# A first quarter of x loaded a second time for its statistics, GpSimd's shuffles with the lower half first, and a new order of the work on every engine

## The chip, the cores and the metric

The kernel runs on one core of one Trainium2 chip. The metric is device time in microseconds (us) of one execution, inputs and output in HBM. Lower is better.

## The reference

One block of a sequence model, with S = 2048 positions and D = 448 channels, all inputs bf16. A long convolution over the sequence is done by FFT, its result gates the normalized input, and an MLP that mixes positions follows.

```python
def _A_ref(q, k, v, shift_k, ssm_k, ssm_D):          # q = layernorm(x)
    k_shift = sum(k_pad[:, t:t+S, :] * shift_k[:, 3-t] for t in range(4))
    kv  = k_shift * v
    y   = irfft(rfft(pad(kv)) * rfft(pad(ssm_k)))[:S]   # length 2S, along the sequence
    return q * (y + kv * ssm_D)

def _B_ref(x, w1, b1, w2, b2):                        # F = 1792, positions are mixed
    u = gelu(einsum("bsd,sf->bdf", layernorm(x), w1) + b1)
    return (einsum("bdf,fs->bds", u, w2) + b2).transpose(0, 2, 1)

x  = A_q
h  = x + _A_ref(layernorm(x), A_k, A_v, A_shift_k, A_ssm_k, A_ssm_D)
h2 = h + _B_ref(layernorm(h), B_w1, B_b1, B_w2, B_b2)
```

## The kernel before

**Layout.** A position s is 16*q + r: q is the partition (128 of them), r the row (16). x, k, v and the output lie in one arena of SBUF as 16 rows of 448 channels per partition. PSUM has 8 banks, and the FFT stages take them in pairs.

**Stages,** by the names that the kernel gives them (its `PLAN`):

- `tables` computes the sine tables; `loads` brings ssm_k, k, v and small vectors; `kT` and `kv.0` to `kv.8` transpose ssm_k and k on TensorE; `kv.9` to `kv.16` do the four-tap shift with diagonal matrices and multiply by v on VectorE (L983).
- `k1` (ssm_k) and `u1` (kv) are the first FFT stage: 16 steps each of 8 small matmuls (L1035), each evacuated from two PSUM banks to SBUF in one instruction (L1045, or L1043 for the first four of k1). Every second step sends three DMAs that move the data across partitions, here called shuffles: two from GpSimd's queue (8 partitions each) and one from SP's (16 partitions), L1051.
- `k2` and `u2` are the second FFT stage (L1070, evacuated at L714 to L718).
- `i1` multiplies the two spectra: 16 products on VectorE, 128x1792 each (L1136), and does the first inverse stage on TensorE (L1153); its results are evacuated (L714) and shuffled once more: two DMAs from GpSimd (lower and upper half of the partitions, L1176) and two from SP (two further rows) for each of seven pairs. The last pair, `i1.16`, goes out by four DMAs of its own: three on SP's queue and one on ScalarE's (L1165).
- `i2` is the second inverse stage, one pair of matmuls for each row r (L1275; rows 0 and 1 have four more, L1283). On its result the gate, both normalizations and the result Q of a row are worked out by VectorE, ScalarE and GpSimd.
- `mlp.0` to `mlp.15` multiply the first half of w1 by Q row by row (L1408, 7 matmuls a row, between the i2 matmuls); `mlp.17` to `mlp.23` the second half (L1418); `mlp.24` to `mlp.39` are w2 and the output (L1430).

Beside these run `xload` (x in four quarters, L891), `q` (mean and variance of each row of x, `bn_stats` at L1212, then `bn_aggr` at L1214, and two small GpSimd instructions for 1/sqrt), `xn` (rows 0 to 3 normalized by ScalarE, L1245), `ct` (transposes of the tables for i2), and `w1a`, `w1b`, `w2` (the weights, by SP). The four quarters of x land in the place of the shuffles' ring buffers, so they can't start before the last u1 shuffle has landed: that is `after=shuf["u"]` in `emit_xload`. `w1a.0` has that condition too; `w1a.1` to `w1a.3` wait for the four DMAs of `i1.16`.

**Order.** Each engine runs one list, written out in `ORDER`. A token such as `u2.11:4-5` means the operations 4 and 5 of step 11 of stage u2. `_Sched.schedule` replays the lists with a model of durations, which decides the interleaving in which waits are placed and which PSUM bank each step takes; the order on an engine is the list's. An engine never runs ahead of an instruction that waits.

**Names used below.** `i1.16:9` and `i1.16:18` evacuate the last inverse pair (both on ScalarE); `i1.16:19`, `:20`, `:22` are its DMAs on SP, `i1.16:21` the one on ScalarE. `i1.4:17` is the evacuation ahead of the last two GpSimd shuffles, `i1.4:18` and `i1.4:20`. `i2.1`, `i2.2`, `i2.9`, `i2.10` are rows 0 and 1 of the second inverse stage, `i2.17` row 2, the first whose data come from `i1.16`'s DMAs; `i2.3` to `i2.8` turn row 0 into Q, for which `mlp.0` waits.

The pieces of code that matter most:

```python
def emit_xload():
    for c in range(4):
        op("sp", lambda e, W, c=c: e.dma_start(X[:, 4*c:4*c+4, :], x2d[:, 4*c:4*c+4, :]),
           w=[(o_X + 4*c*DB, 4*DB)], dmab=128*4*DB, after=shuf["u"])
# emit_q, for each row r
op("dve", lambda e, W, bs=bs, r=r: e.bn_stats(out=bs, in_=X[:, r, :]), r=[(o_X + r*DB, DB)], w=[(ob, 24)], n=D, kind="1x")
```

Of the kernel before, what the change touches and what calls it, by code (L numbers as in the profile page):

```python
# [10 lines left out]
ENGS = ("pe", "act", "dve", "pool", "sp")  # L11
# [3 lines left out]
        "kT.3:9-11 kT.5:0-7 kT.2:4-7 kT.5:9-10 kT.6:0-7 kT.7:0-7 bias.0:0 kT.5:11 kv.7:0-7 k1.8:0-7 k1.9:0-7 "  # L15
        "k1.12:0-7 k1.10:0-7 kv.1:0-7 kv.2:0-11 k1.11:0-7 k1.15:0-7 k1.14:0-7 k1.13:0-7 kT.4:0-7 kv.8:0-11 "
        "kv.12:0-23 kv.9:0-27 kv.10:0-23 kv.11:0-27 k1.4:0-7 k1.0:0-1 u1.0:0-7 k1.0:2-7 u1.1:0-7 u1.2:0-7 k1.1:0-7 "
        "u1.3:0-7 kv.13:0-27 u1.4:0-7 k1.5:0-7 kv.14:0-23 k1.6:0-7 u1.6:0-7 k1.2:0-7 u1.5:0-7 kv.15:0-27 k1.7:0-7 "
        "u1.7:0-7 u1.8:0-7 u1.9:0-7 k1.3:0-7 k2.0:0-3 k2.1:0-3 k2.12:0-3 k2.13:0-3 k2.4:0-3 k2.5:0-3 kv.16:0-23 "
        "k2.9:0-3 k2.8:0-3 u1.10:0-7 u1.12:0-7 u1.13:0-7 u1.14:0-7 u1.15:0-7 u1.11:0-7 k2.2:0-3 k2.3:0-3 k2.6:0-3 "  # L20
        "k2.7:0-3 k2.10:0-3 k2.11:0-3 k2.15:0-3 k2.14:0-3 u2.0:0-3 u2.1:0-3 u2.13:0-3 u2.12:0-3 u2.8:0-2 u2.9:0-3 "
        "u2.8:3 u2.7:0-3 u2.6:0-3 i1.1:1-7 i1.1:10-16 i1.1:8 i1.1:17 i1.14:10-16 i1.14:1-7 i1.14:17 i1.14:8 "
        "i1.8:1-7 i1.8:10-17 i1.8:8 ct0.0:0-7 u2.10:0-3 u2.11:0-3 i1.10:1 i1.10:10-17 i1.10:2-8 u2.4:0-3 u2.5:0-3 "
        "i1.12:1-8 i1.12:10-17 u2.3:0-3 u2.2:0-3 i1.6:1-8 i1.6:10-17 u2.15:0-3 u2.14:0-3 i1.4:9-15 i1.4:0-7 i1.4:16 "
        "i1.16:1-7 i1.16:10-17 i1.16:8 ct.1:0-7 ct.0:0-7 ct.2:0-7 warm.0:0 i2.1:0-1 i2.2:0-3 i2.9:0-1 i2.10:0-3 "
        "i2.17:0-1 i2.45:0-1 i2.32:0-1 i2.20:0-1 i2.54:0-1 i2.28:0-1 warm.1:0 i2.41:0-1 mlp.0:1 mlp.0:4 mlp.0:2 "
        "mlp.0:0 mlp.0:6 mlp.0:3 i2.58:0-1 mlp.0:5 mlp.1:6 mlp.1:5 mlp.1:4 mlp.1:1 mlp.1:0 mlp.1:3 mlp.1:2 "
        "i2.67:0-1 mlp.2:3 mlp.2:2 mlp.2:1 mlp.2:5-6 mlp.2:4 mlp.2:0 mlp.3:4-5 mlp.3:2 mlp.3:1 mlp.3:3 mlp.3:0 "
        "mlp.3:6 i2.71:0-1 mlp.4:4 mlp.4:2 mlp.4:1 mlp.4:5 mlp.4:3 mlp.4:6 mlp.4:0 i2.80:0-1 mlp.5:1-2 mlp.5:4 "
        "mlp.5:6 mlp.5:5 mlp.5:0 mlp.5:3 i2.84:0-1 mlp.6:0 mlp.6:6 mlp.6:1 mlp.6:5 mlp.6:2 mlp.6:4 mlp.6:3 "  # L30
        "i2.93:0-1 mlp.7:6 mlp.7:0-1 mlp.7:5 mlp.7:3-4 mlp.7:2 mlp.8:2 mlp.8:6 mlp.8:5 mlp.8:3-4 mlp.8:0-1 mlp.9:3 "
        "mlp.9:1 mlp.9:6 mlp.9:0 mlp.9:5 mlp.9:4 mlp.9:2 i2.97:0-1 mlp.10:3 mlp.10:0 mlp.10:2 mlp.10:4-6 mlp.10:1 "
        "mlp.11:0 mlp.11:3 mlp.11:2 mlp.11:5 mlp.11:4 mlp.11:6 mlp.11:1 mlp.12:4 mlp.12:1 mlp.12:3 mlp.12:5 "
        "mlp.12:0 mlp.12:6 mlp.12:2 mlp.13:5 mlp.13:2 mlp.13:0 mlp.13:6 mlp.13:3 mlp.13:1 mlp.13:4 mlp.14:3 "
        "mlp.14:0 mlp.14:2 mlp.14:1 mlp.14:5 mlp.14:4 mlp.14:6 mlp.15:5 mlp.15:1 mlp.15:6 mlp.15:0 mlp.15:3 "
        "mlp.15:2 mlp.15:4 mlp.17:0-15 mlp.18:0-15 mlp.19:0-15 mlp.20:0-15 mlp.21:0-15 mlp.22:0-15 mlp.23:0-15 "
# [18 lines left out]
        "tables.7:7 kv.5:8 kT.5:8 kT.2:8 kT.7:8 kT.6:8 bias.1:0 kv.7:8 k1.12:8 kv.1:8 kv.2:12 kv.0:4 kT.4:8 kv.8:12 "  # L55
        "kv.12:24-25 kv.9:28-29 kv.10:24-25 kv.11:28-29 k1.0:8 k1.1:8 u1.3:8 kv.13:28-29 kv.14:24-25 k1.2:8 "
        "kv.15:28-29 u1.7:8 k1.3:8 k2.1:5 k2.5:4 kv.16:24-25 k2.9:5 u1.10:8 u1.11:8 k2.3:4 k2.7:4 k2.11:5 k2.15:5 "
        "u2.1:5 i1.0:0 i1.1:0 i1.14:0 i1.13:0 i1.7:0 i1.8:0 i1.9:0 i1.10:0 ct0.0:8 q.1:2 q.1:0 i1.11:0 i1.12:0 "
        "q.1:1 q.1:3 u2.5:5 i1.5:0 q.2:0 i1.6:0 i1.3:0 i1.2:0 q.2:1-2 q.3:0 i1.15:0 xn.0:1 q.2:3 i1.16:0 q.3:2 "
        "q.3:1 q.3:3 q.5:0 q.5:2 q.5:1 q.4:2 q.5:3 q.7:0 q.4:0 q.4:3 q.4:1 q.7:2 xn.3:1 q.6:0 q.6:2 q.6:1 q.6:3 "  # L60
        "i2.3:0 i2.4:0 i2.11:0 i2.5:0 i2.18:0 i2.6:0 i2.12:0 i2.21:0 i2.13:0 i2.8:0 i2.14:0 i2.55:0 i2.30:0 i2.16:0 "
        "i2.34:0 i2.43:0 i2.26:0 q.7:3 q.7:1 i2.47:0 i2.27:0 q.8:2 q.8:0 q.8:3 q.8:1 i2.39:0 i2.56:0 i2.40:0 "
        "i2.73:0 i2.60:0 i2.69:0 i2.52:0 i2.82:0 i2.85:0 i2.53:0 i2.86:0 i2.65:0 i2.66:0 i2.78:0 i2.79:0 i2.95:0 "
        "i2.98:0 i2.99:0 i2.92:0 i2.91:0 i2.105:0 i2.104:0 mlp.24:14 mlp.25:14 mlp.26:14 mlp.27:14 mlp.28:14 "
        "mlp.29:14 mlp.30:14 mlp.31:14 mlp.32:14 mlp.33:14 mlp.34:14 mlp.35:14 mlp.36:14 mlp.37:14 mlp.38:14 "
        "mlp.39:14 mlp.39:30 "
# [110 lines left out]
class _Sched:  # L177
# [50 lines left out]
    def op(self, W, fn, r=(), w=(), br=(), bw=(), n=0, kind=None, est=None, dmab=None, keng=16, rate=None, after=(), safter=(), mode=0):  # L228
# [3 lines left out]
        o = _Op()  # L232
# [90 lines left out]
    def schedule(self):  # L323
        ops = self.ops
        n = len(ops)
# [23 lines left out]
        free_at = {e: 0.0 for e in ENGS}  # L349
        fab = 0.0  # L350
        mode = 0
        events = []
        t = 0.0
        done = 0
        finish = [0.0] * n
        start = [0.0] * n
        INF = 1e18

        def can_acquire(o):
            need = {}  # L360
            for b in o.acq:
                need[b.pool] = need.get(b.pool, 0) + b.k
# [196 lines left out]
def _build(nc, A_q, A_k, A_v, A_shift_k, A_ssm_k, A_ssm_D, B_w1, B_b1, B_w2, B_b2, out):  # L559
# [11 lines left out]
    DB = 2 * D  # L571
# [921 lines left out]
```

## Time and profile before

| | us |
|---|---|
| median of the runs shown | 175.15 (174.36 to 175.57) |
| the profiled execution, its own time | 173.93 |
| its span | 172.1 |
| from the start to the first product of the spectra | 50.43 |
| from there to the landing of the last shuffle | 28.24 |
| from there to the end of the span | 93.4 |

| engine | busy us | share of the span | instructions |
|---|---|---|---|
| TensorE (PE) | 161.4 | 94% | 1419 |
| VectorE (DVE) | 102.7 | 60% | 190 |
| ScalarE (ACT) | 90.1 | 52% | 130 |
| GpSimd (POOL) | 59.0 | 34% | 152 |

Busy time is an average over stages with different limits; the stages are read one by one below. A matmul in the profile is counted busy from its issue to its modelled end, so that matmuls overlap: one of 448 columns is shown at about 0.35 us, and the next starts 0.19 us after it. Evacuations that follow each other overlap in the same way: one of 128x896 lasts 0.91 us on ScalarE and 1.08 on VectorE, and the next begins 0.80 and 1.00 us after it.

### The profile page before, as it was taken

The page shows a single profiled execution, that of the slowest core. Times are in us where ns is not written, and L with a number is a line of the kernel's source. Part 1 is how long each engine was busy: PE and PEld are TensorE (multiplying, and loading weights), DVE is VectorE, ACT ScalarE, POOL GpSimd, SP SyncE. Part 2 cuts the span into 40 slices and gives each one's busy share as a digit, 9 for nine tenths or more (in the row PEclk, how much of TensorE's full clock was granted, in tenths as well). Part 3 has the DMA queues.
Part 4 walks back from the last instruction along what each step waited for, and adds up shares of the span by engine and source line. Part 5 has one row for each costly group of instructions (what it writes and reads, how often), then busy time and mean ns, then how long its engine had stood idle before and what let it go on. Part 6 is the DMA issues. An engine that isn't in the chain of part 4 may idle for free.

```text
span 172.1 us, 3562 instructions
## 1 busy us (share of the span) xinstructions
PE 161.4 (94%) x1419; PEld 93.4 (54%) x1419; DVE 102.7 (60%) x190; ACT 90.1 (52%) x130; POOL 59.0 (34%) x152
## 2 busy tenths in 40 slices
PE   6999999979999998759999999999999999999994
PEld 2676745433333433333454555555567777777783
DVE  7998899868979999999999550000003132132231
ACT  3696757798999999989958345421210000000000
POOL 8344817690820546664898740000000000000000
PEclk9999999999999999999999999999999999999999
DMA  5999765783749677655599999993000111101111
GB/s 157 416 289 386 275 203 212 298 333 127 224 109 342 251 195 240 200 170 145 162 363 396 403 421 424 411 425 157 0 0 4 53 53 53 53 0 57 53 53 53
DMA packets 15628, 35.15 MB, mean 204 GB/s; under 512 B 3740, under 2 KB 9740, under 8 KB 15612
## 3 DMA queue, kind: packets, MB, share of 16 engines
q1 hardware_dynamic: 12468, 28.25, 45.1%
q0 software_dynamic: 2880, 6.49, 12.0%
q8 instruction: 11, 0.18, 0.4%
q10 hardware_dynamic: 264, 0.18, 0.3%
q14 instruction: 5, 0.04, 0.1%
HBM read 22.05 MB, written 1.84 MB: 139 GB/s over the span
## 4 chain that ended last, share of the span: by engine, by line
PE 63%; DMA 12%; ACT 9%; DVE 8%; issue 2%; POOL 2%; SPq 1%; DVEq 0%; POOLq 0%
PE ps L1430 24%; PE ps L1408 12%; PE ps L1418 12%; DMA arena<-arena 7%; ACT arena L714 6%; DVE arena L1136 6%; DMA arena<-in_A_ssm_k_dram 5%; PE ps L1035 4%; PE ps L1275 3%; ACT arena L1045 2%; POOL arena L1051 2%; PE ps L1070 2%; PE ps L968 2%; PE ps L1014 2%; DVE arena L983 2%
## 5 line engine op out<-in xcount | busy, mean ns | idle before, releaser
L1433 DVE SCALAR_TENSOR_TENSOR arena<-ps,arena 128x448 bf16<-128x448 f32 (+2 forms) x17 | 11.1, 656 | 56.2 <-PE ps L1430 56.2
L1430 PE MATMUL ps<-arena 128*128 128x448 bf16 (+2 forms) x238 | 42.7, 342 | 0.0
L1430 PEld LDWEIGHTS ps<-arena 128*128 128x128 bf16 x238 | 33.3, 145 | 9.5
L714 ACT CAST arena<-ps 128x896 bf16<-128x896 f32 (+1 forms) x31 | 25.0, 955 | 0.6 <-PE ps L911 0.3
L1045 ACT CAST arena<-ps 128x896 bf16<-128x896 f32 x23 | 19.5, 913 | 6.7 <-PE ps L1035 5.9
L1408 PE MATMUL ps<-arena 128*128 128x448 bf16 x112 | 22.5, 353 | 0.0
L1051 POOL DMA_DIRECT2D arena<-arena x32 | 17.5, 553 | 12.4 <-ACT arena L1045 11.8
L1418 PE MATMUL ps<-arena 128*128 128x448 bf16 x112 | 21.4, 352 | 0.0
L1398 ACT ACTIVATE arena<-ps,arena 128x448 bf16<-128x448 f32 x14 | 8.3, 637 | 18.1 <-PE ps L1418 14.4
L1136 DVE TENSOR_TENSOR arena<-arena 128x1792 bf16<-128x1792 bf16 x16 | 16.6, 1085 | 1.0 <-DMA arena<-arena 0.9
L1070 PE MATMUL ps<-arena 128*64 128x448 bf16 x128 | 15.5, 360 | 1.8 <-DMA arena<-arena 1.0
L1153 PE MATMUL ps<-arena 64*128 64x448 bf16 x128 | 14.9, 351 | 2.1 <-POOL arena L1232 0.9
L1418 PEld LDWEIGHTS ps<-arena 128*128 128x128 bf16 x112 | 11.0, 98 | 10.2
L1408 PEld LDWEIGHTS ps<-arena 128*128 128x128 bf16 x112 | 10.8, 98 | 10.6 <-DVE arena L1361 0.7
L1035 PE MATMUL ps<-arena 128*32 128x448 bf16 x256 | 15.1, 355 | 0.6 <-DVE arena L983 0.3
L1176 POOL DMA_DIRECT2D arena<-arena x14 | 8.3, 597 | 13.5 <-ACT arena L714 13.5
L1153 PEld LDWEIGHTS ps<-arena 64*128 64x128 f16 x128 | 5.9, 94 | 10.9 <-DVE arena L1136 3.7
L1070 PEld LDWEIGHTS ps<-arena 128*64 128x64 f16 x128 | 5.7, 108 | 10.7 <-ACT arena L715 2.6
L1275 PE MATMUL ps<-arena 128*128 128x448 bf16 x32 | 8.0, 353 | 2.1 <-DMA arena<-arena 1.9
L1330 ACT ACTIVATE arena<-arena 128x448 bf16<-128x448 f32 x14 | 8.0, 574 | 3.3 <-DVE arena L1302 3.1
L1035 PEld LDWEIGHTS ps<-arena 128*32 128x32 f16 x256 | 5.0, 95 | 8.4 <-DVE arena L983 2.6
L983 DVE TENSOR_TENSOR arena<-ps,arena 128x512 bf16<-128x512 f32 (+1 forms) x16 | 9.0, 617 | 0.8 <-PE ps L968 0.8
(96 smaller groups left out, 191.0 us busy)
## 6 DMA issues: line engine op xcount, KB each, us to landing
arena<-in_B_w_dram SPq DMA_DIRECT2D x8, 896.0 KB, 7.0
arena<-in_B_w_dram SPq DMA_DIRECT2D x2, 2048.0 KB, 17.0
arena<-arena SPq DMA_DIRECT2D x16, 224.0 KB, 3.4
arena<-arena POOLq DMA_DIRECT2D x32, 112.0 KB, 3.3
arena<-in_B_w_dram SPq DMA_DIRECT2D x2, 1536.0 KB, 19.1
arena<-arena POOLq DMA_DIRECT2D x14, 196.0 KB, 4.4
arena<-in_A_k_dram SPq DMA_DIRECT2D x4, 448.0 KB, 6.1
arena<-in_A_v_dram SPq DMA_DIRECT2D x4, 448.0 KB, 9.0
```

The source lines that it names most:

```text
L714: return e.copy(out=dst(), in_=src())
L983: return e.tensor_tensor(out=v, in0=u.rearrange("p t (r d) -> p t r d", d=64), in1=v, op=ALU.mult)
L1035: op("pe", lambda e, W, b=b, r=r, q=q, x=x, c0=c0: e.matmul(PS[32 * q:32 * q + 32, b.slots[x], 0:D], E[:, 2 * r + x, c0:c0 + 32], src[:, r ...
L1045: return e.copy(out=dst, in_=Ppair(b)) if W == "act" else e.tensor_copy(out=dst, in_=Ppair(b))
L1051: shuf[tag].append(op(q_, lambda e, W, g=g, i=i, a=a, nu=nu, jh=jh: e.dma_start(T[a + i:a + i + 4 * nu - 3:4].rearrange("p (j k) c d -> p ...
L1070: op("pe", lambda e, W, b=bs[h], h=h, j=j, c=c, par=par: e.matmul(PS[64 * par:64 * par + 64, b.slots[c], 0:D], FW[:, 64 * c:64 * c + 64], ...
L1136: op("dve", lambda e, W, m=m, i=i: e.tensor_tensor(out=MR(m.slots[0]).rearrange("p (x y) d -> p x y d", x=2), in0=TU[:, i].unsqueeze(2).br ...
L1153: k = op("pe", lambda e, W, b=bs[h], m=ms[h], par=par, t=t, tab=tab, xy=xy, P=P: e.matmul(Pb(b, par), tab[P, :], MR(m.slots[0])[P, xy, :], ...
L1275: k = op("pe", lambda e, W, b=b, r=r, h=h: e.matmul(Pb(b), ET[:, 2 * r + h, :], TZ[:, r, h, :], start=(h == 0), stop=(h == 1 and r >= NZ)) ...
L1408: op("pe", lambda e, W, r=r, fc=fc, b=bs[fc]: e.matmul(Pb(b), W1A[:, r, 128 * fc:128 * fc + 128], Q[:, r, :], start=(r == 0), stop=(r == R ...
L1418: op("pe", lambda e, W, r=r, fc=fc, b=b: e.matmul(Pb(b), W1B[:, r, 128 * (fc - n0):128 * (fc - n0) + 128], Q[:, r, :], start=(r == 0), sto ...
L1430: op("pe", lambda e, W, r=r, fc=fc, b=b, d0=d0, d1=d1: e.matmul(Pb(b)[:, d0:d1], W2[fc // 7][:, fc % 7, r:S:R], G[:, fc, d0:d1], start=(fc ...
```

## The change

1. A new stage `xe` loads the first quarter of x (rows 0 to 3, 448 KB) a second time, early, into rows 8 to 11 of the place of k, which are dead once k is transposed. The `bn_stats` of rows 0 to 3 read this copy; everything else still reads x where it was.
2. The lists of `ORDER` are new for all five engines, from about 12 us of the profile on. What moves:
   - from VectorE to ScalarE: the evacuations `kT.6:8`, `kv.8:12`, `u1.3:8`, `u1.7:8`, and the gates `i2.85:0`, `i2.98:0`; from ScalarE to VectorE: `k1.7:8`, `u2.11:5`, `i1.16:9`.
   - the `bn_stats` of rows 0 to 2 to between `k1.1:8` and `kv.13` (three in a row), that of row 3 to behind `u1.11:8`, with their `bn_aggr`.
   - GpSimd: `k1.11` ahead of `k1.9`, `k1.15` ahead of `k1.13`, `u1.3` ahead of `k1.5` and `k1.1`, `u1.15` ahead of `u1.11` (which was split around it); in i1 the lower half goes out first in every pair, `i1.1` leads, and the small instructions of rows 0 to 3 stand ahead of or among the first pairs.
   - SP: `xe.0` behind the first four shuffles; x's quarters in the order 2, 3, 1, 0; `i1.8` and `i1.10` early; `i1.16:20`, `:19`, `:22` in the place of `:22`, `:19`, `:20`; `w1a.0` behind `i1.16` and `i1.12:20` (it was behind the first two quarters of x); the left-over shuffles of i1 ahead of `w1a.1` to `w1a.3`, which follow each other.
   - TensorE: the order of a few steps in the first 16 us and in k2, u1, u2; `i2.41` ahead of `i2.54` and `i2.32`; the order of the seven matmuls in each row of the MLP.
3. The model in `schedule` has new constants for DMAs and latencies. It has no effect on the lists; it can change the bank that a step takes.

```diff
+        NE = 4
+        o_XE = o_KH + 8 * DB
+        XE = view(o_XE, [NE, D])
+        def emit_xearly():
+            for c in range(NE // 4):
+                sch.t0 = c
+                op("sp", lambda e, W, c=c: e.dma_start(XE[:, 4 * c:4 * c + 4, :], x2d[:, 4 * c:4 * c + 4, :]),
+                   w=[(o_XE + 4 * c * DB, 4 * DB)], dmab=128 * 4 * DB)
...
-                    op("dve", lambda e, W, bs=bs, r=r: e.bn_stats(out=bs, in_=X[:, r, :]), r=[(o_X + r * DB, DB)],
+                    op("dve", lambda e, W, bs=bs, r=r: e.bn_stats(out=bs, in_=XE[:, r, :] if r < NE else X[:, r, :]),
+                       r=[(o_XE + r * DB if r < NE else o_X + r * DB, DB)],
                        w=[(ob, 24)], n=D, kind="1x")
...
     "dve": (
-        ... k1.0:8 k1.1:8 u1.3:8 kv.13:28-29 kv.14:24-25 k1.2:8 kv.15:28-29 u1.7:8 k1.3:8 k2.1:5 k2.5:4 kv.16:24-25 k2.9:5 u1.10:8 u1.11:8 ...
-        ... i1.9:0 i1.10:0 ct0.0:8 q.1:2 q.1:0 i1.11:0 i1.12:0 q.1:1 q.1:3 u2.5:5 i1.5:0 q.2:0 i1.6:0 i1.3:0 i1.2:0 q.2:1-2 q.3:0 i1.15:0 xn.0:1 q.2:3 i1.16:0 q.3:2 ...
+        ... k1.0:8 k1.1:8 q.2:0 q.1:2 q.1:0 kv.13:29 kv.13:28 kv.14:25 kv.14:24 k1.2:8 k1.7:8 kv.15:29 kv.15:28 k1.3:8 k2.1:5 k2.5:4 kv.16:24-25 k2.9:5 u1.10:8 q.1:3 q.1:1 u1.11:8 q.2:2 q.2:1 ...
+        ... i1.10:0 i1.9:0 ct0.0:8 u2.11:5 i1.11:0 i1.12:0 u2.5:5 i1.5:0 i1.6:0 q.3:2 xn.0:1 i1.3:0 i1.2:0 xn.3:1 q.3:0 i1.15:0 i1.16:0 q.4:2 q.4:0 q.3:1 q.3:3 i1.16:9 ...
     "sp": (
-        ... k1.15:11 u1.1:11 ... xload.1:0 xload.0:0 w1a.0:0 xload.2:0 ct0.1:0-1 ... i1.16:22 i1.16:19-20 i1.12:22 i1.6:22 w1a.1:0 i1.4:21 ...
+        ... k1.15:11 xe.0:0 u1.1:11 ... xload.2:0 xload.3:0 ct0.1:1 ct0.1:0 xload.1:0 xload.0:0 ... i1.16:20 i1.16:19 i1.16:22 i1.12:20 w1a.0:0 i1.6:20 i1.6:22 i1.12:22 i1.14:22 i1.14:20 i1.1:20 i1.1:22 w1a.1:0 w1a.2:0 w1a.3:0 i1.4:21 ...
```

## The prediction

> **What bounds the kernel now.** I read the page first, then the chain of work that ended last, then busy time by stage. The chain shows who sets the end (start, length, engine, line; all in us).
>
> ```profile
> 46.25 4.15 DMA arena<-arena
> 50.41 0.02 issue
> 50.43 1.10 DVE arena L1136
> ...
> 59.26 1.06 DVE arena L1212 x2
> ...
> 62.50 3.17 ACT arena L714 x4
> 65.67 0.01 issue
> 65.69 4.87 ACT arena L714 x6
> ...
> 75.17 3.50 DMA arena<-arena
> 78.67 0.05 issue
> 78.72 0.94 PE ps L1275 x4
> ```
>
> Until 50.43 us the path runs through evacuations and shuffles and ends with the last u1 shuffle (4.15 us to land). Then VectorE (two of the moved `bn_stats` lie on the path), ScalarE's evacuations, the last shuffle of `i1.16` (landing at 78.67), and from there TensorE.
>
> ```profile
> 50.40:72.50 22.10, 19.81 (x176) 8.07 (x176) 22.02 (x32) 21.97 (x28) 9.39 (x18) 1.00 0.75 237
> 72.50:82.00 9.50, 7.43 (x54) 3.91 (x54) 8.99 (x29) 8.37 (x13) 5.40 (x11) 1.00 0.55 164
> 82.00:106.00 24.00, 24.00 (x128) 12.23 (x127) 17.23 (x48) 14.24 (x36) 15.96 (x38) 1.00 0.95 356
> ```
>
> The columns are length, then busy time of PE, PEld, DVE, ACT, POOL, the granted clock, the DMA share and GB/s. From 50.4 to 72.5 VectorE and ScalarE are both full, and TensorE nearly. From 82 to 106 TensorE alone is full: what comes after the first MLP matmul (81.86) is fixed. The time moves only by when `mlp.0` can start, and by stalls behind it.
>
> **Leg A, up to the first product (50.43).** The three `bn_stats` put behind `k1.1:8` take 3 x 0.53 us (the spacing of the pair at 59.18) of VectorE. Between 25.9 and 36.5 VectorE idles 1.8 us in all and loses `u1.3:8` and `u1.7:8` (1.00 each) for `k1.7:8` (1.00): room for 2.8, so they fit in total. But they stand ahead of `kv.13:29`. By my walk along the new lists with the durations of the old rows, `k1.1:8` ends at 26.99 (27.19 before), `kv.13:29` starts at 28.5 (28.11), `k1.2:8` ends at 31.7 (31.68), `k1.7:8` at 32.9 (33.71), `kv.15:28` at 34.5 (33.52), `k1.3:8` at 35.5 (35.73). `k2.0` waited for the landing of `k1.5:10` at 35.43; now it waits for `k1.1:10`, eighth in the same run of GpSimd's issues (issue about 31.0 against 30.67). So k2 starts 0 to 0.4 later by the issue, and up to 0.8 earlier if the landing takes nearer 4 than 4.76 us. From there both evacuating engines repeat the old lists. `u1.11:8` comes earlier (TensorE no longer waits for `u1.15`), and its `bn_aggr` and `bn_stats` (0.2 + 0.6) lie in the 0.8 us that VectorE idled before 43.21. The last GpSimd shuffle, `u1.11:10`, comes behind `u1.15`'s two, which wait for its evacuation at 44.51: 44.8 and three more issues of 0.54 is 46.4, against 46.25. Leg A: +0.1, bounds -0.8 (the last shuffle lands in 3.35 us like `u1.11:9`, not in 4.15) and +0.6.
>
> What the reordering must hide: GpSimd issues `k1.9` behind `k1.11` now, `k1.9:10` at about 21.2 instead of 18.00. `k1.0:8` (24.9) refills that buffer. Shuffles of that stretch land in 2.97 to 4.37 us, so at 24.2 to 25.6: a loss of 0 to 0.7 at VectorE, of which the 0.5 us before `k2.0` covers part (inside the +0.6).
>
> **The early load.** It is issued behind `k1.15:11`, at about 22.4 (`k1.15:8` now ends near 21.8, because ScalarE has `kv.8:12`, 0.90). VectorE asks for it at 26.9, so 4.5 us are free. The same 448 KB have a row:
>
> ```profile
> DMA to landing us min/median/max: 3.6/4.6/7.1
> ```
>
> Those are the four quarters of x. I take 4.3 (the second of them, issued beside another load): no stall. The bounds are 3.6 (nothing) and 7.1 (2.6 us of stall at the head of VectorE's queue, with `kv.13` and all of k1's and u1's evacuations behind it). [...]
>
> **Leg B, from the first product to the landing of `i1.16`.** Out of VectorE's list ahead of `i1.16:0` go five `bn_stats` (rows 0 to 3 and one of row 4), four `bn_aggr`: 1.09 + 0.16 + 0.54 + 0.60 + 0.53 + 0.09 = 3.0 us by the starts of what follows each. In come `u2.11:5` (1.07, as `u2.5:5`), two `bn_stats` of rows 4 and 5 (1.06) and a small one (0.1): 2.2. ScalarE loses `u2.11:5` (0.80). But TensorE hands out work no faster here: `i1.10:8` ends at 61.17 and `u2.5` at 62.05 in both. So ScalarE gains 0.4, not 0.8 (`u2.5:4` at 62.10, 62.50 before); from there its ten further evacuations run 0.80 apart, and `i1.4:17` starts at 70.17 (70.48). `i1.15:0` waits for `u2.15:4`, `i1.16:0` follows and ends at 70.95 (71.46): -0.5.
>
> Behind it, before: `i1.16:18` and `:9` in a row on ScalarE, the latter ending 2.97 us after `i1.16:0`; SP issues two more DMAs, and the last lands at 7.21. Now: `i1.16:9` on VectorE, behind two `bn_stats` and two `bn_aggr` (1.2), ends at 2.3. But SP's list has its two DMAs first and `:22` third: 2.33 + 2 x 0.71 + an issue to landing of 3.5 = 7.25. The parallel evacuation is eaten by the order of SP's queue. GpSimd's last pair follows `i1.4:17` (-0.3), lands at 75.8 (76.12), and TensorE's twelve matmuls of rows 0 and 1 then end just as `i1.16` lands. Leg B: -0.5, bounds -0.9 and 0.
>
> [...] GpSimd's issues in this stage last 587 to 666 ns beside two-input products, against 544 in the median in k1 and u1: 0.05 each, nothing on the path, and the last pair follows the last product. [...]
>
> **Leg C, up to `mlp.0`.** Row 0's Q is a chain: `i2.2` ends, three instructions on VectorE, one on GpSimd, then `i2.8`.
>
> ```profile
> 77.52 0.68 DVE L1312 SCALAR_TENSOR_TENSOR arena<-ps,arena 128x448 f32<-128x448 f32 x1 [0.47 <-PE ps L1283]
> ...
> 79.36 0.17 DVE L1321 BATCH_NORM_AGGREGATE arena<-arena 128x2 f32<-128x6 f32 x1
> ...
> 80.26 0.55 POOL L1354 TENSOR_TENSOR arena<-arena 128x1 f32<-128x1 f32 x1 [1.76 <-DVE arena L1350]
> ...
> 81.31 0.48 DVE L1361 TENSOR_SCALAR arena<-arena 128x448 bf16<-128x448 f32 x1
> ```
>
> It starts 0.3 earlier (77.2, after the pair's landing). The second `i2.11:0` now waits to 78.4 for row 1, and one `bn_aggr` more stands ahead of `i2.8`, which ends at 81.6 (81.80). TensorE, with the same 15 matmuls between `i2.17` and `mlp.0`, is ready at 81.4 and waits. So 0.3 of leg B's 0.5 is given back. And `w1a.0`, moved past 16 issues of SP (two quarters of x, six small ones of `ct0`, eight shuffles), is issued at about 76.1 instead of 51.28: 5.5 us before it is needed. Its kind lands in 4.8 to 6.35 us (`w1a.1` to `w1a.3`; it had a cover of 24 us before): from nothing to +0.85. I take 4.8, that of `w1a.1`, which was also issued behind small shuffles. `w1a.1` goes out at 81.5 (78.69) behind seven issues of 0.71, lands by 86.3 to 87.9, and `mlp.4` needs it at 88.0: just covered.
>
> **Sum.** A +0.1, B -0.5, C +0.3: -0.1; the MLP adds nothing. The profiled execution took 173.93 (span 172.1 and 1.8 around it), which becomes 173.8. The runs' median is 1.2 above that execution, so I forecast 175.0.
>
> **Rivals.**
> - *Landings and gaps fall well* (A -0.8, B -0.9, C half given back): -1.0 to -1.8, 173.2 to 174.1. For it: ScalarE and VectorE are full in B and lose 0.8 each. Against: the chain changes hands within 0.4.
> - *`w1a.0` comes late.* It decides when its landing exceeds 5.5 us; 6.2 is the median of its line. +0.5 to +0.9: 175.6 to 176.0.
> - *The early load stops VectorE* (slower). Place: `q.2:0` ahead of `kv.13`. It decides from a landing of 4.5 us. At the rows' 7.1 us, `kv.15:28` ends at 37.1, `k2.0` starts 1.7 later, and the whole path with it; with `k1.9:10` late as well 2.2: 176.7 to 177.3. Against: the DMA share is 0.76 there, not full.
> - *The change doesn't relieve the path at all*: B 0, C 0, because TensorE hands out the work at the old times; +0.1, 175.2.
>
> **How the numbers follow.** Forecast and the last rival together 0.58 (0.46 and 0.12), well-falling landings 0.16, `w1a.0` 0.13, the early load 0.13. About 1% (1.75 us) is what a measurement can tell from no change. Faster by more needs all of the first rival: 0.09. Slower by more is the early load and the tail of `w1a.0`: 0.15. The range takes in the first rival's middle and the foot of the third: 173.6 to 176.6.
>
> **What would show it.** The first product still near 50.5; `bn_stats` gone from 59 to 69 but two; `i1.16:0` ending at 71.0; the last landing at 78.2; TensorE idle 0.3 to 0.5 before `mlp.0` and nowhere behind it. Wrong if VectorE idles at 27 waiting for a DMA, if `mlp.0` or `mlp.4` waits for w1, or if the first product moves by over 0.8.

## The result, and the profile after

The changed kernel takes 176.01 us (median of 20 runs, 174.46 to 177.40) against 175.01 for the kernel before: a ratio of 1.0064, 95% interval 1.0039 to 1.0089. It is slower by 1.0 us, 0.6%, where no change was forecast (175.0); the time is inside the range of 173.6 to 176.6. The ratios here and below leave out runs more than 1.5% above the fastest of their kernel (one of these 20, and five of the twelve of after_w1a, a variant below). The profiled execution took 176.74 us (span 174.9), 2.8 more than that of the kernel before. So 1.8 of the 2.8 belongs to these two executions and not to the change; the first task is to tell the two apart.

Part of it is there from the start: `kv.12`, the first of TensorE's shift steps, begins at 19.92 us here and at 19.43 before, ahead of the early load's issue (22.55). In the 18 profiles of this document that start lies between 19.12 and 20.78, so two profiles can differ by half a us in absolute times without any effect of what comes later.

The chain of work that ended last, of the changed kernel (start, length, engine, line; us):

```profile
22.55 6.20 DMA arena<-in_A_q_dram
29.32 1.14 DVE arena L1248 x2
...
49.60 9.82 ACT arena L739 x12
...
70.20 1.79 ACT arena L739 x2
72.28 0.58 POOL arena L1212
72.86 3.95 DMA arena<-arena
...
78.85 1.49 PE ps L1320 x4
80.34 1.79 PE ps L1312 x6
...
84.08 0.92 PE ps L1445 x4
```

The early load stands on the path, which it was not to do. It lands 6.20 us after its issue. Then ScalarE's evacuations lead for 10 us without a break, and the last link before the second inverse stage is now a GpSimd shuffle (`i1.4:20`), not one of `i1.16`'s. The four matmuls of L1320 take 1.49 us at 78.85. The first MLP matmul comes at 84.06 (81.86 before).

VectorE around the load (start, length, operation, and the idle time ahead with what ended it):

```profile
26.89 1.08 DVE L1079 TENSOR_TENSOR arena<-ps,arena 128x896 bf16<-128x896 f32 x1
28.77 1.68 DVE L1248 BATCH_NORM_STATS2 arena<-arena 128x6 f32<-128x448 bf16 x3 [0.80 <-DMA arena<-in_A_q_dram]
30.37 0.67 DVE L1019 TENSOR_TENSOR arena<-ps,arena 128x512 bf16<-128x512 f32 x1
```

The kernel before at the same place:

```profile
27.11 1.08 DVE L1045 CAST arena<-ps 128x896 bf16<-128x896 f32 x1
28.11 2.00 DVE L983 TENSOR_TENSOR arena<-ps,arena 128x512 bf16<-128x512 f32 x3
```

VectorE waits 0.80 us for the load, works 1.6 us on statistics, and `kv.13`, whose matmuls end at 28.58, begins behind them at 30.37 (28.11 before). `k2.0` starts at 36.75 (35.47). The shuffles issued beside the load land late too: `k1.15:10` in 6.53 us (3.63 before).

The three stages of the prediction's second view (length, busy time of PE, PEld, DVE, ACT, POOL, granted clock, DMA share, GB/s), and then the same view second by second:

```profile
50.40:72.50 22.10, 20.44 (x183) 8.40 (x184) 21.32 (x26) 21.86 (x28) 10.43 (x18) 1.00 0.66 200
72.50:82.00 9.50, 7.14 (x47) 3.75 (x45) 8.04 (x23) 6.04 (x9) 3.54 (x7) 0.82 0.62 192
82.00:106.00 24.00, 23.77 (x123) 11.34 (x122) 18.09 (x52) 17.00 (x40) 17.07 (x40) 1.00 0.99 370
```

```profile
77.00:78.00 1.00, 1.00 (x7) 0.49 (x5) 0.77 (x3) 1.00 (x2) 0.14 (x1) 1.00 0.53 166
78.00:79.00 1.00, 1.00 (x4) 0.40 (x3) 0.76 (x2) 1.00 (x3) 0.92 (x2) 0.55 0.67 127
79.00:80.00 1.00, 1.00 (x4) 0.46 (x3) 0.55 (x1) 0.77 (x1) 0.22 (x1) 0.50 0.99 315
80.00:81.00 1.00, 1.00 (x4) 0.42 (x3) 0.62 (x2) 0.00 (x0) 0.00 (x0) 0.50 0.96 340
81.00:82.00 1.00, 1.00 (x6) 0.43 (x5) 0.88 (x5) 0.22 (x1) 0.04 (x1) 0.74 0.57 215
```

The granted clock reads 0.82 where it was 1.00. In fact it is 0.50 from 78.1 to 81.5, and the matmuls of rows 0 to 3 follow each other after 0.37 us instead of 0.19. Ahead of it TensorE idled for the last shuffle, here and, for less time, in the kernel before:

```profile
76.85 0.55 PE L1312 MATMUL ps<-arena 128*128 128x448 bf16 x2 [2.36 <-DMA arena<-arena]
```

```profile
76.17 0.55 PE L1275 MATMUL ps<-arena 128*128 128x448 bf16 x2 [1.90 <-DMA arena<-arena]
```

Row 0's chain is late by all of this; the lines that answer to those of before:

```profile
78.20 0.68 DVE L1349 SCALAR_TENSOR_TENSOR arena<-ps,arena 128x448 f32<-128x448 f32 x1 [0.43 <-PE ps L1320]
...
80.98 0.17 DVE L1358 BATCH_NORM_AGGREGATE arena<-arena 128x2 f32<-128x6 f32 x1
...
83.52 0.48 DVE L1398 TENSOR_SCALAR arena<-arena 128x448 bf16<-128x448 f32 x1
```

Q of row 0 is done at 84.00. `w1a.0` landed at 83.69, so in this execution its lateness is hidden behind the lower clock and nobody waits for it.

### The profile page after: what moved, and what is told of

Read it like the earlier page. It is cut to its first block, busy times and chain, and to the rows that moved or that the text cites. A ratio compares the mean times of both kernels' runs of the same rounds, so it can differ in the third digit from the quotient of the medians.

```text
span 174.9 us, 3563 instructions
## 1 busy us (share of the span) xinstructions
PE 163.5 (93%) x1419; PEld 94.1 (54%) x1419; DVE 102.0 (58%) x187; ACT 92.3 (53%) x133; POOL 59.9 (34%) x152
## 4 chain that ended last, share of the span: by engine, by line
PE 62%; ACT 13%; DMA 10%; DVE 9%; POOL 2%; issue 1%; SPq 1%; DVEq 0%; POOLq 0%
PE ps L1467 24%; PE ps L1445 12%; PE ps L1455 12%; ACT arena L739 9%; DMA arena<-in_A_k_dram 5%; PE ps L1106 4%; DMA arena<-in_A_q_dram 4%; PE ps L1312 3%; ACT arena L1081 3%; PE ps L1071 3%; DVE arena L1172 2%; DMA arena<-arena 2%; DVE arena L1019 2%; PE ps L1320 1%; DVE arena L742 1%
## 5 line engine op out<-in xcount | busy, mean ns | idle before, releaser
L1467 PEld LDWEIGHTS ps<-arena 128*128 128x128 bf16 x238 | 33.3, 145 | 9.5
L1081 ACT CAST arena<-ps 128x896 bf16<-128x896 f32 x24 | 20.5, 912 | 5.9 <-PE ps L1071 5.8
L739 ACT CAST arena<-ps 128x896 bf16<-128x896 f32 (+1 forms) x29 | 23.2, 923 | 0.6 <-PE ps L1189 0.2
L1445 PE MATMUL ps<-arena 128*128 128x448 bf16 x112 | 22.7, 353 | 0.0
L1455 PE MATMUL ps<-arena 128*128 128x448 bf16 x112 | 21.4, 352 | 0.0
L1312 PE MATMUL ps<-arena 128*128 128x448 bf16 x32 | 9.0, 390 | 2.6 <-DMA arena<-arena 2.4
L1329 ACT ACTIVATE arena<-ps,arena 128x448 f32<-128x448 f32 x11 | 7.6, 722 | 4.5 <-PE ps L1312 3.0
```

Of the source, the lines that this page charges most:

```text
L739: return e.copy(out=dst(), in_=src())
L1081: return e.copy(out=dst, in_=Ppair(b)) if W == "act" else e.tensor_copy(out=dst, in_=Ppair(b))
L1312: k = op("pe", lambda e, W, b=b, r=r, h=h: e.matmul(Pb(b), ET[:, 2 * r + h, :], TZ[:, r, h, :], start=(h == 0), stop=(h == 1 and r >= NZ)) ...
L1445: op("pe", lambda e, W, r=r, fc=fc, b=bs[fc]: e.matmul(Pb(b), W1A[:, r, 128 * fc:128 * fc + 128], Q[:, r, :], start=(r == 0), stop=(r == R ...
L1455: op("pe", lambda e, W, r=r, fc=fc, b=b: e.matmul(Pb(b), W1B[:, r, 128 * (fc - n0):128 * (fc - n0) + 128], Q[:, r, :], start=(r == 0), sto ...
L1467: op("pe", lambda e, W, r=r, fc=fc, b=b, d0=d0, d1=d1: e.matmul(Pb(b)[:, d0:d1], W2[fc // 7][:, fc % 7, r:S:R], G[:, fc, d0:d1], start=(fc ...
```

## The experiments

Three suspects stand: the clock drop, the early load with its three statistics, and the weight load `w1a.0`. In the names, "aw" is the kernel after and "bw" the kernel before, each with the warm matmuls of the first experiment. Every kernel has 12 runs; 35 runs of the kernel before were made beside each set of four on the same chip. A "drop" is a run whose mean clock reads below 0.997, and "full" is the median of the others. The interval is that of the ratio to the kernel before.

| kernel | median | before | ratio (95%) | full | drops |
|---|---|---|---|---|---|
| after_warm | 175.63 | 175.04 | 1.0054 (1.0019 to 1.0088) | 175.63 | 0 |
| before_warm | 174.05 | 175.04 | 0.9977 (0.9944 to 1.0009) | 174.05 | 0 |
| after_gaps | 175.63 | 175.04 | 1.0059 (1.0029 to 1.0089) | 175.56 | 2 |
| after_noload | 175.25 | 175.04 | 1.0044 (1.0013 to 1.0076) | 174.80 | 7 |
| aw_w1a | 174.53 | 175.13 | 0.9984 (0.9953 to 1.0015) | 174.48 | 1 |
| aw_i14 | 175.54 | 175.13 | 1.0023 (0.9992 to 1.0054) | 175.38 | 2 |
| aw_all | 174.67 | 175.13 | 0.9966 (0.9940 to 0.9992) | 174.68 | 0 |
| bw_w1a_late | 174.48 | 175.13 | 0.9963 (0.9935 to 0.9990) | 174.48 | 0 |
| after_same | 176.36 | 175.36 | 1.0077 (1.0042 to 1.0113) | 175.99 | 7 |
| after_w1a | 176.08 | 175.36 | 1.0009 (0.9966 to 1.0052) | 174.76 | 7 |
| before_warm2 | 174.10 | 175.36 | 0.9943 (0.9908 to 0.9977) | 174.10 | 0 |
| aw_w1a_i14_noload | 174.04 | 175.36 | 0.9933 (0.9905 to 0.9960) | 174.04 | 0 |
| before_warm3 | 174.25 | 175.21 | 0.9969 (0.9938 to 1.0000) | 174.25 | 0 |
| bw_w1a_late2 | 174.77 | 175.21 | 0.9991 (0.9954 to 1.0028) | 174.76 | 0 |
| bw_w1a_later | 175.50 | 175.21 | 1.0026 (0.9996 to 1.0056) | 175.50 | 0 |
| aw_xe_first | 175.01 | 175.21 | 1.0005 (0.9973 to 1.0037) | 174.94 | 2 |

The kernel before itself has drops in 75 of its 140 runs; by the medians each costs 1.2 to 1.5 us (for instance 174.42 full and 175.85 with a drop, beside after_same). The changed kernel has them in 11 of its first 20 runs (176.27, against 175.21 without) and in 7 of the 12 of after_same.

### The clock: warm matmuls in TensorE's idle time

```diff
-N_WZ, N_WI, N_W0, N_WK, N_WJ = 2, 0, 9, 3, 0
+N_WZ, N_WI, N_W0, N_WK, N_WJ = 11, 0, 9, 3, 0       # 9 in the kernel before
-  ... ct.2:1-7 i2.1:0-1 ...
+  ... ct.2:1-7 warm.1:0 ... warm.9:0 i2.1:0-1 ...   # before: warm.0:0 warm.1:0 ... warm.7:0 i2.1:0-1
```

> The changed kernel with nine more matmuls on data that nobody reads, put between the transposes of the tables and the first row of the second inverse stage, where TensorE idled for 2.36 us (74.49 to 76.85). Clock theory: in the profile of the changed kernel the granted clock is 0.50 from 78.3 to 81.4, right behind that idle time, and eleven of its twenty runs have a mean clock of 0.99 (median 176.27) against nine of 1.00 (median 175.21). If the idle time sets the clock down, all runs now have 1.00, and the median falls from 176.0 to about 175.2 with a narrower spread. Rival (the clock falls for another reason, or costs nothing on the path): the median stays at 176.0 within 0.3 and runs at 0.99 remain.

> The kernel before with seven more such matmuls in its idle time of 1.90 us (74.27 to 76.17). Its twenty runs lie from 173.9 to 176.5, too wide for one state. Clock theory: its upper runs have the same drop, its clean ones are those below 175; the median falls from 175.0 to 174.2 to 174.5 and no run is above 175.2. Rival (no clock drop in the kernel before, the spread is something else): 175.0 within 0.3.

> The kernel before with seven warm matmuls once more, beside the others on one chip: all runs at full clock, 0.7 to 1.0 below the kernel before by the means. Rival (the first time was the chip): within 0.3 of the kernel before.

> The kernel before with seven warm matmuls, as the foot of the next two on the same chip: 0.6 to 1.0 below the kernel before, all runs at full clock.

TensorE in before_warm3, where eight warm matmuls (one was there before) now fill part of the idle time:

```profile
73.63 1.68 PE L1185 MATMUL ps<-arena 128*128 128x448 f16 x8
76.60 0.55 PE L1274 MATMUL ps<-arena 128*128 128x448 bf16 x2 [1.29 <-DMA arena<-arena]
```

The kernel before gains 0.96 to 1.26 in the median on three chips, with no drop in 36 runs; the interval excludes no change on one chip, ends at it on the second and takes it in on the third. One of its runs without a drop, 175.34, lies above the expected limit of 175.2. So the clock theory holds for the drops of both kernels, and for the median of the kernel before. But the drops are as frequent before (75 of 140) as after (18 of 32), so they are not why the change is slower. With the drops gone from both, the difference is not smaller but larger: 175.63 against 174.05, 1.58 us (1.35 by the two ratios). after_warm fell less than expected (175.63, not 175.2) and still spreads from 174.66 to 176.52, and its profile shows what is left at `mlp.0`: TensorE stands still for 1.37 us more than a matmul's step, until 83.34, Q of row 0 having been ready at 82.38 and `w1a.0` landing at 83.25.

### The early load: statistics in the gaps, no load, an earlier load

```diff
 # after_gaps, VectorE's list
-  k1.1:8 q.2:0 q.1:2 q.1:0 kv.13:29 ... k1.7:8 kv.15:29 ... k2.1:5 k2.5:4 ... k2.9:5 u1.10:8
+  k1.1:8 kv.13:29 ... k1.7:8 q.1:0 kv.15:29 ... k2.1:5 q.2:0 k2.5:4 ... k2.9:5 q.1:2 u1.10:8
 # after_noload
-  ("xe", emit_xearly, ()),                          # and xe.0:0 out of SP's list
 # aw_xe_first (with warm matmuls, w1a.0 and i1.4 as below), SP's list
-  k1.9:11 k1.11:11 k1.13:11 k1.15:11 xe.0:0
+  k1.9:11 k1.11:11 xe.0:0 k1.13:11 k1.15:11
```

> The changed kernel with its three early bn_stats no longer in a row ahead of kv.13, but one each behind k1.7:8, k2.1:5 and k2.9:5, where VectorE idles. Early-load theory (the wait of 0.80 us for the load at 27.97 and 1.6 us of statistics ahead of kv.13 put k2 and the evacuations 1.25 us back): no wait at 28, kv.13:29 at 28.6 (30.37), k2.0 at 35.6 to 36.0 (36.75), u2.1:4 on ScalarE at 48.5 to 48.8 (49.60), first product at 50.3 to 50.5 (50.84), and the time 0.4 to 0.9 below the changed kernel's. Clock theory alone: the time falls by no more than 0.3, because the idle time before row 0 and its clock drop stay.

> The changed kernel without the early load: the statistics of rows 0 to 3 read what is left of k in the same place, so they are not those of x, and nothing is loaded twice. Early-load theory: the wait of 0.80 us is gone, the shuffles of k1.13 and k1.15 land in 3 to 4.4 us (6.0 to 6.5 beside the load), kv.13:29 starts at 29.4 (30.37), k2.0 at 35.8 to 36.1, the time falls by 0.3 to 0.7. Rival (the place of the three statistics costs, not the load): kv.13:29 still 1.3 later than before, k2.0 at 36.3 or later, the time falls by less than 0.3.

> The changed kernel with warm matmuls, w1a.0 and the last pair of i1.4 back in time, and the early load issued ahead of the shuffles of k1.13 and k1.15 instead of behind them, at about 20.0 instead of 22.6. Early-load theory: it lands at 25.5 to 26.5, VectorE has no wait for it at 26 to 28 and kv.13:29 starts at 28.9 to 29.3, so 0.3 to 0.6 below the same kernel with the load in its place (174.5 to 174.6 by the runs so far) and near the one without the load (174.0). Rival (the place of the three statistics, and the shuffles that the load slows, make the loss): no better than 174.5.

In after_gaps the wait and the statistics are gone from the path: `kv.13:29` at 28.27, `k2.0` 1.1 earlier and what follows 0.8 to 1.0 earlier (its `kv.12` begins at 19.93, as in the changed kernel), the first product at 49.84 (50.84), `i1.16:0` ending at 70.86 (71.68). Yet the time fell little: by 0.4 in the median, by 0.1 in the ratio. Its `w1a.0`, issued 0.8 earlier with everything else (76.10), landed at 82.73, and `mlp.0` waited 1.45 us for it. So this run doesn't tell what the wait at VectorE costs.

after_noload has no such wait at VectorE:

```profile
26.89 1.67 DVE L1247 BATCH_NORM_STATS2 arena<-arena 128x6 f32<-128x448 bf16 x3
28.47 2.20 DVE L1018 TENSOR_TENSOR arena<-ps,arena 128x512 bf16<-128x512 f32 x4
```

The time fell by 0.8 in the median and 0.35 in the ratio, whose interval overlaps that of the changed kernel. `k2.1:5` starts 1.2 earlier than in the changed kernel, of which 0.5 is there from the start (`kv.12` at 19.40). The shuffles of `k1.15` and `k1.13` that took 6.0 to 6.5 us beside the load (from `k1.15:10` on) land in 4.2 to 4.7. And here the prediction's walk of leg A comes true: `kv.13:29` at 28.47 (28.5 forecast), `k1.2:8` ending at 31.67 (31.7), `k1.7:8` at 32.89 (32.9), `u1.11:10` issued at 46.49 (46.4). The walk was right; the load that it took as covered was not.

Issued 3 us earlier, the load does land early (24.64), but VectorE is worse off (aw_xe_first):

```profile
27.40 2.09 DVE L1078 TENSOR_TENSOR arena<-ps,arena 128x896 bf16<-128x896 f32 x2 [2.41 <-DMA arena<-arena]
29.41 1.67 DVE L1247 BATCH_NORM_STATS2 arena<-arena 128x6 f32<-128x448 bf16 x3
```

Now `k1.0:8` waits for the shuffle `k1.9:10`, issued at 21.12 behind the load and landing at 27.38 (6.26 us; 3.6 to 3.9 in the two kernels without the load). The early-load theory, as a matter of the load's own landing, falls here (174.94 at full clock, where 173.9 to 174.3 was expected; the same kernel with the load in its old place was not run), and the rival holds: the shuffles beside the load land late, those of `k1.15` and `k1.13` (6.0 to 6.5 us) with the load in its old place, `k1.9:10` with the load moved. In aw_i14 (below) it landed as late as 30.34, 8.11 us after its issue:

```profile
30.37 1.68 DVE L1247 BATCH_NORM_STATS2 arena<-arena 128x6 f32<-128x448 bf16 x3 [2.77 <-DMA arena<-in_A_q_dram]
```

VectorE waited 2.77 us, TensorE idled for 2.9 us until 33.3, and the clock read 0.50 from 33.9 to 37.3: 178.60 us for that run. With warm matmuls, so without the drop ahead of row 0, the four kernels with the load and the three statistics in a row have 5 drops in 48 runs, and those without the load none in 84; aw_all, with the load and the statistics in the gaps, has none in 12.

### The weight load w1a.0

```diff
 # aw_w1a, after_w1a: SP's list (aw_: with the nine warm matmuls)
-  xload.2:0 xload.3:0 ct0.1:1 ... i1.16:22 i1.12:20 w1a.0:0 i1.6:20
+  xload.2:0 xload.3:0 w1a.0:0 ct0.1:1 ... i1.16:22 i1.12:20 i1.6:20
 # aw_i14: w1a.0 as in the change
-  i1.1:22 w1a.1:0 w1a.2:0 w1a.3:0 i1.4:21 i1.4:19
+  i1.1:22 i1.4:21 i1.4:19 w1a.1:0 w1a.2:0 w1a.3:0
 # aw_all: both, and the statistics of after_gaps
```

> The changed kernel with the nine warm matmuls, and w1a.0 back behind the first two quarters of x on SP's queue. Weight theory: with the clock full, mlp.0 waits 1.37 us for the landing of w1a.0 (83.25, 6.56 after its issue), and i2.93 waits 1.07 us for i1.4:19 (95.24), which lands last in a queue of w1a.0 to w1a.3. So mlp.0 starts when i2.8 is done, at 82.0 to 82.4 (83.34); w1a.1 to w1a.3 and i1.4:19 land 2 us earlier, i2.93 waits no longer, and the time falls by 1.2 to 2.0 against the changed kernel with warm matmuls alone (175.63). Early-load theory (what was lost at VectorE before 37 us is what the end shows): the time falls by at most 0.3.

> The changed kernel with the nine warm matmuls, and i1.4:21 and i1.4:19 ahead of w1a.1 instead of behind w1a.3; w1a.0 stays where the change put it. Weight theory: the wait of 1.37 us before mlp.0 stays, that of 1.07 before i2.93 goes; w1a.1 is issued 1.4 later and lands at 89.5 to 91, so that mlp.4 (89.77) may wait up to 1 us for it: the time falls by 0.2 to 1.0 against 175.63. Early-load theory: no change beyond 0.2.

> The changed kernel with all four repairs: warm matmuls, w1a.0 back, i1.4:21 and i1.4:19 ahead of w1a.1, and the three early bn_stats in VectorE's gaps. Weight theory: first product at 49.6 to 49.9, i1.16:0 ending at 70.9, mlp.0 at 81.6 to 81.9, i2.93 without a wait, so no worse than the kernel before with warm matmuls (174.05): 173.4 to 174.1. Early-load theory: the gain in the first part shows in full, 0.6 below the kernel before with warm matmuls, with the weights making no difference between this and the changed kernel with warm matmuls and spread statistics.

> The changed kernel as it is, as the foot of the next three on the same chip: 1.0 us (0.6%) above the kernel before, about half of its runs with a mean clock of 0.99.

> The changed kernel with one edit: w1a.0 back behind the first two quarters of x. Weight theory: the runs with full clock no longer wait about 1.4 us before mlp.0 and come down by 0.9 to 1.2; in runs with the clock drop Q of row 0 is late itself, so they gain less (0.3 to 0.8); the median falls by 0.6 to 1.1 and stands within 0.3 of the kernel before. Rival (the early load and the clock make the loss): at most 0.3.

TensorE in after_same, an execution of the changed kernel at full clock, and then in aw_w1a:

```profile
81.51 1.11 PE L1311 MATMUL ps<-arena 128*128 128x448 bf16 x5
83.81 0.92 PE L1444 MATMUL ps<-arena 128*128 128x448 bf16 x4 [1.19 <-DVE arena L1330]
```

```profile
81.27 0.54 PE L1311 MATMUL ps<-arena 128*128 128x448 bf16 x2
82.12 0.93 PE L1444 MATMUL ps<-arena 128*128 128x448 bf16 x4 [0.30 <-DVE arena L1386]
```

The profile puts the first wait down to a VectorE instruction. But Q of row 0 was done at 82.86; what came at 83.72 is the landing of `w1a.0`, 6.57 us after its issue. Put back to its old place, the wait shrinks to 0.30 and `mlp.0` follows `i2.8` (82.06) at once. aw_w1a stands at 174.48 at full clock where after_warm has 175.63 (ratios 0.9984 and 1.0054, on two chips). The intervals of these two ratios don't overlap. On one chip, after_same and after_w1a have 175.99 and 174.76 at full clock: 1.2 us, as expected, though from five runs each, which overlap (175.01 to 177.01 and 173.78 to 175.86). The median of all of after_w1a's runs fell by only 0.3, because three of its seven drops were double ones (mean clock 0.981, 178.5 to 180.3). The early-load theory, by which `w1a.0` would make at most 0.3, falls.

aw_i14 removed the wait of `i2.93` for `i1.4:19` that after_warm's profile had (1.07 us; the load queue of `w1a.0` to `w1a.3` stands ahead of it), but `w1a.1` then came late and `mlp.4` waited 0.72 us in the profile (that of the run of 178.60 us): 0.25 less at full clock and 0.5 less by the ratio, the lower half of what was expected. aw_all has no wait for a weight or a shuffle in the MLP, and 174.67: better than the kernel before (0.9966), but not better than the kernel before with warm matmuls, and 0.6 above the upper end of its forecast (173.4 to 174.1). It isn't better than aw_w1a either (174.53, on the same chip), which has the statistics in a row. So its earlier first product (49.38 in the profile, 50.21 in aw_w1a) shows in the profile's end (span 172.1 against 172.8) and not in the runs, and what VectorE's wait for the load costs the runs is not shown by any pair of runs.

### The same delay in the kernel before

```diff
 # bw_w1a_late, bw_w1a_late2 (before, with the seven warm matmuls), SP's list
-  xload.1:0 xload.0:0 w1a.0:0 xload.2:0 ... i1.16:19-20 i1.12:22 i1.6:22
+  xload.1:0 xload.0:0 xload.2:0 ... i1.16:19-20 i1.12:22 w1a.0:0 i1.6:22
 # bw_w1a_later
+  xload.1:0 xload.0:0 xload.2:0 ... i1.16:19-20 i1.12:22 i1.6:22 i1.4:21 i1.4:19 w1a.0:0 w1a.1:0
```

> The kernel before with its seven warm matmuls and one step of the change: w1a.0 behind i1.16 and one more shuffle instead of behind two quarters of x. Weight theory: issued at about 76, it lands 6.4 to 6.8 later at 82.4 to 83, mlp.0 (81.87) waits 0.6 to 1.2 for it, and w1a.1 to w1a.3 come 2 us later, which mlp.8 may feel: slower than the kernel before with warm matmuls (174.05) by 0.6 to 1.5. Early-load theory: nothing, within 0.2.

> The same with w1a.0 behind i1.16 and one shuffle. Its first profile waits 1.72 us at mlp.0 and starts the second half of w1 1.1 us later, but its runs were only about 0.3 above those of its foot, on another chip. Weight theory: beside its foot it is 0.6 to 1.2 slower. Rival (the wait is made good in most runs, by a shorter landing or by slack behind it): 0.0 to 0.4 slower.

> The same with w1a.0 behind three more shuffles, so issued 2.1 us later, at about 78.3. Weight theory: mlp.0 waits 3.3 to 3.9 us, 2.0 more than with one shuffle, and the time rises by 1.6 to 2.4 against that (more if the long idle time sets the clock down). Rival: the slack takes up part, less than 1.0 more.

bw_w1a_late left it unclear: a wait in the profile (1.72 us), no loss in the runs. On one chip there is a loss: 174.25 (foot, before_warm3), 174.77, 175.50, by the means 174.30, 174.94 and 175.55. The first step is small beside the scatter of its runs (173.42 to 175.90, the foot's 173.56 to 174.74); the two together, 1.25, are clear of it: eleven of the twelve runs of bw_w1a_later lie above all of the foot's. The chain of bw_w1a_later names the load itself:

```profile
78.15 5.04 DMA arena<-in_B_w_dram
83.19 0.05 issue
83.24 1.31 PE ps L1407 x6
```

The delay is on the path in the old order too. Both sizes came out smaller than the weight theory had them (0.6 to 1.2, and 1.6 to 2.4 more); the second is within its rival's limit of 1.0. One shuffle: a wait of 1.8 us in the profile (0.33 of it is there without the delay), 0.5 to 0.6 in the runs, since the profiled execution (175.84) is near the slowest of its twelve. Three more shuffles: issued 1.5 later, the load lands in 5.04 us instead of 7.17, and the wait in the profile is no longer, though the runs are 0.6 to 0.7 slower; how long the landing takes in the unprofiled runs isn't known. In these traces `w1a.0` landed 6.1 to 7.2 us after an issue at which shuffles of `i1.16` had not yet landed, and in 5.04 when issued as the last of them landed (here; `w1a.1` in the kernel before and in before_warm3 took 4.8 like this). That what is in flight decides is not shown by that alone: `w1a.1` of the changed kernel, also issued when `i1.16` had landed, took 4.82 in after_same and 7.28 in after_warm.

### Both costs taken out

> The changed kernel with warm matmuls, w1a.0 and the last pair of i1.4 back in time, and without the early load: the statistics of rows 0 to 3 read what is left of k, so they are not those of x. If the loss was the weights plus the wait for the load, the rest of the change is a gain: first product at 49.4 to 49.8, i1.16:0 ending near 70.4, no wait of VectorE at 26 to 28, and the time 0.3 to 0.9 below the kernel before with warm matmuls. If the load costs nothing beyond what the weights do, it equals the changed kernel with warm matmuls and w1a.0 back (0.1 to 0.4 above the kernel before with warm matmuls).

This kernel leaves out the load. First product at 50.05, `i1.16:0` ending at 70.84, no wait of VectorE at 26 to 29; 174.04 against 174.10 for before_warm2 on the same chip. So what is left of the change, the reordered i1 and the parallel evacuation of `i1.16` above all, is worth nothing that these runs can tell (ratios 0.9933 and 0.9943, intervals of about 0.003 to each side), and the expected gain of 0.3 to 0.9 did not come: from the first product to the start of the second half of w1 it takes 56.1 us in both.

## Why the prediction was wrong

**The step that failed is leg C's term for `w1a.0`.** It was seen, its place was right, and its rival gave the mechanism: the landing decides from 5.5 us on. The term was mis-sized: 4.8 was taken, from `w1a.1`, which in the kernel before goes out when the last shuffle has landed. The nearest row was the wrong one; the median of the line, 6.2, was nearer to the measured 6.6 to 6.8. At full clock that is a wait of about 0.9 beyond Q of row 0 (after_same: `w1a.0` issued at 77.15, landed at 83.72, Q ready at 82.86), and 1.2 us in the runs (the rival had +0.5 to +0.9). What the rest of the 1.2 is stays open. The queue behind it is a candidate that "the MLP adds nothing" left out: `w1a.1` to `w1a.3` and `i1.4:19` land 2 to 3 us later in after_warm than in aw_w1a. From the first MLP matmul to the second half of w1 it took 25.0 us in after_warm, but 24.0 in after_same, against 23.9 in the kernel before.

The profile of after_same, an execution at full clock, can be added up against that of the kernel before. It is 0.77 late at `kv.12`, which says nothing of what follows, and from there to the first product 0.13 shorter (leg A: +0.1). From the first product to the first MLP matmul it takes 32.74 us instead of 31.43, where legs B and C had 0.2 less. Of these 1.3 us, 0.9 is the wait for `w1a.0`. The other 0.4 is Q of row 0, mostly because the last GpSimd shuffle, `i1.4:20`, which was to land 0.3 earlier, landed 0.3 later after the first product (in 3.97 us instead of 3.64).

**The early load: 4.3 taken, 6.2 measured.** In the profiles the third rival, which decides from 4.5 on, was right in its mechanism and its place: `k2.0` came 1.28 later than before, 0.8 of it beyond the late start, where its price scaled to 6.2 gives 1.1. "The whole path with it" holds too: against after_noload, with the 0.5 of the start taken off, the changed kernel is 0.7 late at `k2.0`, 0.8 at the first product and 0.7 at the end of `i1.16:0`. That the first product came only 0.41 later than before is because the last shuffle, `u1.11:10`, was issued 1.47 later but landed in 3.10 us instead of 4.15. In the runs the kernels without the load are 0.4 to 0.9 faster (after_noload against the changed kernel; aw_w1a against aw_w1a_i14_noload, on two chips and with one more difference), with intervals that overlap in both pairs. In 5 of the 48 runs with warm matmuls, the load and the three statistics in a row there was a drop, and these took 1.7 to 3.2 more than their kernel's others; the one that was profiled, in aw_i14, is the load landing 8.11 us after its issue, TensorE idle for 2.9 us and the clock at 0.50 for 3.4 us behind that. Issued by SP's queue beside a stage of shuffles, the load took from 5.1 us (aw_xe_first) to 8.1 us (aw_i14) to land.

**Leg A** (+0.1, bounds -0.8 and +0.6) ended inside its bounds, at +0.41 (-0.08 without the late start), but by luck: the load put it back by 0.8, and the short landing of the last shuffle, which the walk had as its lower bound, made that good. **Leg B** (-0.5, bounds -0.9 and 0): -0.12 to the last landing of `i1.16`. ScalarE's part went as worked out (from `u2.1:4` to the end of `i1.4:17` 22.4 us, 23.3 before), but ScalarE began 1.28 later, so the gain was spent on the start. That SP's queue eats the parallel evacuation was right: `:9` ended at 73.99 (74.43) and `:22`, third in the queue, landed at 78.96 (78.67). GpSimd's 14 issues of this stage, beside the products, took 590 to 677 ns, 603 in the mean (587 to 666 and 597 before): the new order made them 6 ns longer in the mean.

**The clock was not in the prediction at all.** The forecast of 175.0 carried it unseen, in the 1.2 us between the profiled execution and the median: 173.93 was a run without a drop, and about half of the runs have one. In the profiled execution it also hides the change's loss: Q of row 0 is late by itself, and `w1a.0` is in time. The runs beside after_same agree: at full clock the change costs 1.57 (175.99 against 174.42), with a drop 0.53 (176.38 against 175.85), and the median shows about the mean of the two. But these are five and seven runs that overlap, and in the first 20 runs a drop costs the changed kernel 1.06, not 0.39, so how much a drop hides is not settled. At full clock the sum of the parts, 1.2 for the weights, 0.4 to 0.9 for the load and nothing for the rest, fits the 1.57 and the 1.58 of the warm pair at its lower end.

Open: why after_w1a had three double drops, which after_same had not; how much of the 1.2 is the wait at `mlp.0` and how much the queue behind it; what decides how long a load takes to land; and how large the early load's part is in the runs.

## What to carry to other kernels

When a load is moved past others in a queue, price its landing by all rows of its kind, those issued with as much in flight first (here 6.1 to 7.2 us beside shuffles of `i1.16`, 5.04 as the last of them landed), and give it the cover of the slow row; the fastest row of its kind is no forecast. When medians lie a constant above the cleanest profile, look for runs with a lower granted clock and at TensorE's longest idle time before dense work: a few matmuls on data that nobody reads took the kernel before from 175.04 to 175.36 down to 174.05 to 174.25 (ratios 0.9977, 0.9943 and 0.9969), below both the kernel before and the changed kernel, and level with the repaired change, aw_all (0.9966). A profile of one execution can hide a wait behind another; compare runs with the same clock with each other before blaming what the chain shows. And before two profiles are compared by absolute times, subtract what they differ by ahead of the change.

## What the runs showed that was not expected

After idle times of 2.4 to 2.9 us in the profiles TensorE's granted clock fell to 0.50 for 3.4 us (78.1 to 81.5 here, 76.0 to 79.4 in after_noload, 33.9 to 37.3 in aw_i14), in some executions of one kernel and not in others (a drop after 2.36 us of idle time here, none after 2.37 us in after_same); the kernel before, whose profile has 1.90 us of idle time, has the lower clock in about half of its runs (75 of 140). What decides between two executions with the same idle time is not shown. With matmuls that left 0.7 to 1.3 us of it (0.7 in aw_all, 1.29 in before_warm3), none of the 12 runs of aw_all and none of the 84 runs of kernels without the load had a drop.
